# Two gated-MLP passes beside attention: ten of twelve f tiles by one level of Strassen's scheme

## The chip, the core and the metric

One core of a Trainium2 chip runs the whole program in one launch. The metric is the device time of one execution in microseconds. TensorE multiplies, VectorE, ScalarE and GpSimd do the rest, SyncE issues most DMAs; instructions on each engine run in the order in which the program holds them, and engines wait for one another by semaphores.

## What is computed

```python
q_s, k_s = q * D**-0.25, k * D**-0.25          # 4 batches, 8 heads, 576 tokens, D = 64
def phi(x):                                     # omega: 128 x 64
    h = einsum('bhsd,md->bhsm', x, omega) - sum(x * x, -1, keepdims=True) / 2
    return exp(h - max(h, -1, keepdims=True)) / sqrt(m)
kv = einsum('bhsm,bhsd->bhmd', phi(k_s), v);  z = sum(phi(k_s), axis=2)
x = einsum('bhsm,bhmd->bhsd', phi(q_s), kv) / (einsum('bhsm,bhm->bhs', phi(q_s), z)[..., None] + 1e-6)
x = x.transpose(0, 2, 1, 3).reshape(2304, 512)
x = ((x @ w_a) * (x @ w_b)) @ w_out             # 512 -> 1536 -> 512
h = maximum(x @ w_in, 0);  out = (h * h) @ w_out2   # 512 -> 2048 -> 512
```

The weights come as 64-bit floats, are read as pairs of 32-bit words and are turned into 32-bit ones on the chip.

## The kernel before

Each large product is done in three matmuls on rounded 32-bit values: an operand is cut into a high and a low part (`TERMS` lists high x high, high x low, low x high). ScalarE casts the high part, VectorE subtracts it from the value for the low part.

The 2304 tokens are nine blocks of 256. The first MLP runs in nine passes (`PASSES`, numbered from 0 here). Passes 0 to 5 take one block each, over half of the twelve f tiles (an f tile is 128 of the 1536 hidden columns); passes 6, 7 and 8 take two blocks each (3 and 4, 5 and 6, 7 and 8) over all f tiles. For an f tile the generator `a_units` yields three units: "a", twelve matmuls with w_a; "b", twelve with w_b, after which ScalarE and VectorE multiply the two results and cut the product; "o", twelve matmuls with w_out into the four y banks (`outs`), for an f tile one or two behind. In passes 6 and 7 these matmuls have 512 columns (`abw`, line 696, and `y`, line 721) and use PSUM banks 4 and 5 for w_a and w_b, 0 to 3 for y; attention has banks 6 and 7.

Attention runs beside passes 0 to 7. `SIDES` says which of its lanes go with which pass; after each unit the main loop advances them by their share. A k lane (`k_steps`, `kt_steps`) makes phi(k) and kv for one batch, a q lane (`q_steps`, `qt_steps`) makes phi(q), the quotient and the columns of x that a later pass reads. `x_all` holds two blocks, `x_mid` (from pass 6 on) blocks 5 and 6. A scheduler then sets the order of the instructions on each engine, from the order in which the program issues them and from what each needs. GpSimd issues the small loads of the last 64 tokens of each head (`kt`, `qt`, `VT`) and does nothing else after the start. w_a and w_b are all in SBUF, cut, by the end of pass 2, and w_out is kept cut in DRAM (`wo_d`) and loaded again per f tile.

The second MLP (from 634.7 us) follows the same cutting, in a scheme of seven products already; its phases are not changed but for addresses.

## Time and profile before

| | |
|---|---|
| time, median of 3 runs | 988.3 us (987.8 to 988.34) |
| profiled execution, first to last instruction | 988.2 us |
| TensorE / VectorE / ScalarE / GpSimd busy | 969.0 / 662.4 / 534.1 / 28.9 us |
| passes 3, 4, 5 | 46.0, 41.2, 42.3 us |
| passes 6, 7, 8 | 124.6, 118.2, 101.1 us |
| phases of the second MLP | 175.0 and 178.5 us |

The passes begin at 41.67, 87.42, 126.49, 161.29, 207.29, 248.47, 290.79, 415.38 and 533.55 us, each at its first matmul with w_a. Busy time of TensorE is counted to the modelled end of each matmul, so a row of starts tells more of its pace than busy time does.

### The profile page before, as it was taken

To read this page: it belongs to the slowest core of one execution; us is meant where nothing else is said; L and a number is where in the kernel's file an instruction comes from. 1 tells how busy PE (TensorE), PEld (TensorE's weight loads), DVE (VectorE), ACT (ScalarE), POOL (GpSimd) and SP (SyncE) were. 2 spreads that over 40 slices of the span, in tenths; PEclk is the share of its full clock that TensorE was granted. 3 is DMA by queue.
4 is the path that set the end of the run, shared out by engine and by line. 5 is a ranking of instruction groups with operands and counts; after the bars stand their busy time and mean duration, and the time that the engine had idled before them with its cause. 6 is when DMAs were issued, how large, how long until landed. Compare 5 with 4: busy or idle time off the path is not lost.

```text
span 988.2 us, 17329 instructions
## 1 busy us (share of the span) xinstructions
PE 969.0 (98%) x6337; PEld 890.0 (90%) x6337; DVE 662.4 (67%) x1624; ACT 534.1 (54%) x1288; POOL 28.9 (3%) x54
## 2 busy tenths in 40 slices
PE   7899999999999999999999999999999999999998
PEld 6799998999998878788888888899999999999998
DVE  3888679765544444444443998988787347988794
ACT  5876556666554533243333554676676555455561
POOL 4000100000000000000000000000000000000000
PEclk9999999999999999999999999999999999999999
DMA  7766976634553111232123999337675599844301
GB/s 188 216 177 199 296 240 210 205 100 137 156 155 101 62 57 54 70 96 76 54 65 128 310 331 362 104 107 233 215 237 200 181 363 407 355 154 145 112 18 49
DMA packets 110358, 171.07 MB, mean 173 GB/s; under 512 B 27713, under 2 KB 83521, under 8 KB 107841
## 3 DMA queue, kind: packets, MB, share of 16 engines
q1 hardware_dynamic: 108736, 168.39, 51.1%
q0 software_dynamic: 1536, 1.58, 0.6%
q8 instruction: 50, 0.82, 0.3%
q14 instruction: 36, 0.29, 0.1%
HBM read 120.13 MB, written 49.81 MB: 172 GB/s over the span
## 4 chain that ended last, share of the span: by engine, by line
PE 78%; DVE 8%; DMA 7%; ACT 5%; issue 2%; SPq 0%; ACTq 0%; DVEq 0%
PE abw L696 14%; PE y L721 10%; PE pY L1026 9%; PE oY L1184 7%; PE ab L696 7%; PE oW L1184 5%; PE pW L1026 5%; PE oX L1184 4%; PE ps_n L548 3%; PE pX L1026 2%; PE ps_kv L482 2%; PE ps_p L329 2%; PE ps_p L404 2%; DMA raw<-in_moe_w_b_dram 2%; PE ps_qt L539 2%
## 5 line engine op out<-in xcount | busy, mean ns | idle before, releaser
L696 PE MATMUL abw<-x_all,W 128*128 128x512 f32 x576 | 142.6, 395 | 0.0
L721 PE MATMUL y<-gs,wo 128*128 128x256 f32 (+1 forms) x720 | 138.1, 332 | 0.2 <-ACT wo L199 0.2
L696 PEld LDWEIGHTS abw<-x_all,W 128*128 128x128 f32 x576 | 105.7, 188 | 20.5
L721 PEld LDWEIGHTS y<-gs,wo 128*128 128x128 f32 x720 | 108.8, 189 | 11.2 <-ACT wo L199 0.6
L696 PE MATMUL ab<-x_all,W 128*128 128x256 f32 x576 | 87.5, 292 | 1.4 <-DVE W L200 0.9
L696 PEld LDWEIGHTS ab<-x_all,W 128*128 128x128 f32 x576 | 74.8, 189 | 3.0 <-DVE W L200 1.5
L696 PE MATMUL abw<-x_mid,W 128*128 128x512 f32 x288 | 71.2, 395 | 0.0
L696 PEld LDWEIGHTS abw<-x_mid,W 128*128 128x128 f32 x288 | 52.5, 188 | 10.4
L415 DVE CUSTOM_DVE_ANT_0 c<-ps_p,c 128x128 f32<-128x128 f32 x152 | 38.3, 286 | 25.0 <-ACT c L413 24.2
L802 ACT CAST gs<-a_s 128x256 fp32r<-128x256 f32 x84 | 33.0, 407 | 30.4 <-DVE a_s L801 29.2
L413 ACT COPY c<-ps_p 128x256 f32<-128x256 f32 x76 | 27.8, 372 | 36.6 <-PE ps_p L404 36.2
L1026 PE MATMUL pY<-W,M 128*128 128x384 f32 x240 | 45.9, 335 | 0.0
L801 DVE TENSOR_TENSOR a_s<-abw,a_s 128x256 f32<-128x256 f32 x48 | 18.1, 419 | 38.2 <-PE abw L696 38.2
L1184 PE MATMUL oW<-W 128*128 128x256 f32 x360 | 43.0, 276 | 0.0
L1026 PEld LDWEIGHTS pY<-W,M 128*128 128x128 f32 x240 | 41.9, 188 | 0.4 <-ACT F L1035 0.3
L1184 PEld LDWEIGHTS oW<-W 128*128 128x128 f32 x360 | 41.8, 188 | 0.2 <-DVE W L1152 0.2
L1151 ACT CAST W<-F 128x384 fp32r<-128x384 f32 x57 | 29.0, 513 | 23.5 <-PE oX L1184 10.6
L696 PE MATMUL ab<-x,W 128*128 128x256 f32 x288 | 41.3, 287 | 0.0
L800 ACT ACTIVATE a_s<-abw 128x256 f32<-128x256 f32 x48 | 17.4, 387 | 42.6 <-PE abw L696 42.5
L1043 ACT ACTIVATE F<-F 128x384 f32<-128x384 f32 x48 | 24.5, 518 | 24.8 <-DVE F L1038 24.7
L548 PEld LDWEIGHTS ps_n<-kvr,qT 128*128 128x128 f32 x256 | 32.3, 191 | 5.9 <-ACT qT L543 3.3
L420 ACT ACTIVATE qp<-c,nm 128x128 f32<-128x128 f32 x88 | 31.0, 397 | 11.4 <-DVE nm L415 10.3
(212 smaller groups left out, 2146.0 us busy)
## 6 DMA issues: line engine op xcount, KB each, us to landing
wo<-wo_d SPq DMA_DIRECT2D x60, 512.0 KB, 3.6
s_d<-F SPq DMA_DIRECT2D x24, 768.0 KB, 5.6
raw<-in_moe_w_out_dram SPq DMA_DIRECT2D x32, 256.0 KB, 4.7
raw<-in_moe_w_in_dram SPq DMA_DIRECT2D x16, 512.0 KB, 6.4
W<-wo_d SPq DMA_DIRECT2D x4, 2048.0 KB, 14.9
F<-s_d SPq DMA_DIRECT2D x5, 1536.0 KB, 7.8
raw<-in_moe_w_a_dram SPq DMA_DIRECT2D x12, 512.0 KB, 3.8
raw<-in_moe_w_b_dram SPq DMA_DIRECT2D x12, 512.0 KB, 5.2
```

Of the source, the lines that this page charges most:

```text
L329: state["proj"] = nc.tensor.matmul(ps[:, 2 * x:2 * x + 2].rearrange("p h m -> p (h m)"), lhsT=s, rhs=OMZ.rearrange("p h m -> p (h m)"), st ...
L413: nc.scalar.copy(out=c, in_=ps[:, :, 1, :])
L415: nc.vector.tensor_tensor_reduce(out=c[:, x, :], in0=ps[:, x, 0, :], in1=c[:, x, :], scale=1.0, scalar=3.0e38, op0=ALU.add, op1=ALU.min, a ...
L420: nc.scalar.activation(out=dst[:, 2 * n + x, :], in_=c[:, x, :], func=ACTF.Exp, scale=-1.0, bias=nm[:, x:x + 1],)
L548: lambda x=x: nc.tensor.matmul(pn[:, x, :], lhsT=t["qT"][:, x % 2 * len(g) + x // 2, :], rhs=kv[:, x % 2, :], start=True, stop=True,)
L696: nc.tensor.matmul(ps, lhsT=wv[:, s_, kc, :], rhs=x[..., kc, m_, :], start=(kc == 0 and (s_, m_) == TERMS[0]), stop=(kc == KC - 1 and (s_, ...
L721: nc.tensor.matmul(y_part(pi, f, c), lhsT=wo[pi, f][:, s_, c * 128:(c + 1) * 128], rhs=g[:, m_, :],  start=(f == f0 and (wide or c % 2 == ...
L802: nc.scalar.copy(out=g[:, 0, c], in_=a_s)
L1026: nc.tensor.matmul(p, lhsT=w[:, s_, 128 * kk:128 * kk + 128], rhs=y[:, ai, kk, m_, :], start=(c not in seen and kk == 0 and (s_, m_) == TE ...
L1043: nc.scalar.activation(out=t[:, o], in_=t[:, o], func=ACTF.Relu)
L1151: ahead_of["cast"] = nc.scalar.copy(out=sop[:, 0], in_=src)
L1184: nc.tensor.matmul(tiles_of(p, t), lhsT=sops[n][:, s_, 128 * t:128 * t + 128], rhs=w[:, m_, :], start=(fresh and k == 0 and (t % 2 == 0 or ...
```

## The change

In passes 6 and 7 the f tiles 0 and 1 run as before. The other ten are taken in pairs (`pair`). For a pair, x is a matrix of 2 x 2 blocks (two token blocks by two halves of the 512 inputs) and the weights one of 2 x 2 (two halves of the inputs by w_a and w_b). One level of the Strassen scheme in Winograd's form gives the four results from seven block products. They need sums of blocks on both sides:

- sums of x (`sums_of_x`): s1, s2, s4, and s3 in place of a block of x, on VectorE and ScalarE while f tiles 0 and 1 run;
- sums of w (`t_made`): four per f tile, by GpSimd in passes 3 and 4, cut by ScalarE and VectorE, stored in DRAM (`t_d`, 1 MB per f tile) and loaded (`t_load`) 512 KB at a time, three buffers, in passes 6 and 7.

The seven products of a pair go through banks 4 and 5 (`sP`, `sR`); each is twelve matmuls of 256 columns. Partial results are copied out or added as they come. The cut product lies in one buffer (`g_mid`). Pools are laid out anew: what only k lanes use is in a pool of its own that closes before pass 6, so all of batch 3's k lane moves into pass 5 (half of it ran in pass 6). Some addresses and pads differ.

```diff
+    def t_made(f):
+        w = seg("W", 8192 * f, 2, 2, 512)
+        full = top["cut"].tile([128, 2, 2, 256], F32, tag="a", name="a")
+        nc.gpsimd.tensor_tensor(
+            out=full.rearrange("p a r n -> p a (r n)"), in0=f32(w[:, :, 0]), in1=f32(w[:, :, 1]),
+            op=ALU.add,
+        )
+        yield
+        b11, b21, b12, b22 = (full[:, a, r] for a in range(2) for r in range(2))
+        t = top["cut"].tile([128, 4, 256], F32, tag="p", name="p")
+        for o, x, y in ((0, b12, b11), (2, b22, b12), (1, b22, t[:, 0]), (3, b21, t[:, 1])):
+            nc.gpsimd.tensor_tensor(out=t[:, o], in0=x, in1=y, op=ALU.subtract)
+        yield
+        o = top["raw"].tile([128, 4, 2, 256], F32R, tag="raw", name="raw")
+        nc.scalar.copy(out=o[:, :, 0], in_=t)
+        nc.vector.tensor_tensor(out=o[:, :, 1], in0=t, in1=f32(o[:, :, 0]), op=ALU.subtract)
+        nc.sync.dma_start(out=t_d[f // 2 - 1][:, :, f % 2], in_=f32(o))
+        yield
...
+        def sums_of_x(x):
...
+            tt(first, u, hi(a21), hi(a22), ALU.add)
+            tt(first, u, u, lo(a21), ALU.add)
+            tt(first, u, u, lo(a22), ALU.add)
+            cut(first, s1, u)
...
+        def pair(pi, f, x, n0):
...
+            prod(p, a11, old(wa, 0), first=True)
+            nc.scalar.copy(out=e1, in_=p)
+            prod(r, s1, new(0), first=True)
+            nc.scalar.copy(out=e5, in_=r)
+            t_load(n0 + 3)
+            yield pi, f, "a"
+            prod(p, s2, new(1))
+            nc.scalar.copy(out=e2, in_=p)
+            t_load(n0 + 4)
+            prod(r, s4, old(wb, 1), last=True)
+            nc.vector.tensor_tensor(out=e2, in0=r, in1=e2, op=ALU.add)
+            yield pi, f, "b"
+            outs(*pending.pop(0))
+            yield pi, f, "o"
+            prod(p, s3, new(2))
+            nc.vector.tensor_tensor(out=e5, in0=p, in1=e5, op=ALU.add)
+            t_load(n0 + 5)
+            r = bank(5, [128, 2, N], "sR")
+            prod(r, a12, old(wa, 1), first=True, last=True)
+            nc.vector.tensor_tensor(out=e1, in0=r, in1=e1, op=ALU.add)
+            nc.vector.scalar_tensor_tensor(
+                out=e1, in0=e1, scalar=1.0 / W_SCALE, in1=e2, op0=ALU.mult, op1=ALU.mult
+            )
+            yield pi, f + 1, "a"
+            prod(p, a22, new(3), last=True)
+            nc.vector.scalar_tensor_tensor(
+                out=e5, in0=p, scalar=1.0 / W_SCALE, in1=e5, op0=ALU.mult, op1=ALU.mult
+            )
+            t_load(n0 + 6)
+            yield pi, f + 1, "b"
+            outs(*pending.pop(0))
...
-        5: lambda: merge(q_lane(2, (0,)), k_lane(3, (0, 1))),
+        5: lambda: merge(q_lane(2, (0,)), k_lane(3)),
         6: lambda: chain(
-            merge(q_lane(2, (1, 2)), k_lane(3, (2, 3))),
+            q_lane(2, (1, 2)),
...
+        if T_FROM <= pi < AT_END - 1 and (kind != "a" or f % 3):
+            next(t_work, None)
```

On TensorE, in pass 7, before: `abw` is a product with w_a or w_b of one f tile, `ps_` names are attention, `y0` and on the w_out product.

```order
L404 MATMUL ps_p_5461<-OM_127,S_5426 128x256 x2
L696 MATMUL abw_5470<-x_mid_3999,W_107 128x512 x12
L561 MATMUL ps_x_5484<-ident_125,xh_5454 128x128 x2
L404 MATMUL ps_p_5490<-OM_127,S_5426 128x256 x2
L696 MATMUL abw_5471<-x_mid_3999,W_107 128x512 x12
L539 MATMUL ps_qt_5524<-ident_125,qp_5459 128x128 x4
L721 MATMUL y0_5431<-gs_5405,wo_5354 128x512 x3
```

The same pass now, the last three products of one pair, then (after the w_out products left out here) the first two of the next:

```order
L580 MATMUL ps_n_5918<-kvr_3793,qT_5890 128x65 x4
L854 MATMUL sP_5810<-x_mid_4268,tsum_5579 128x256 x12
L854 MATMUL sR_5943<-x_mid_4268,W_115 128x256 x12
L436 MATMUL ps_p_5960<-OM_138,S_5913 128x256 x2
L593 MATMUL ps_x_5969<-ident_136,xh_5923 128x128 x2
L854 MATMUL sP_5810<-x_mid_4268,tsum_5838 128x256 x12
...
L854 MATMUL sP_6022<-x_mid_4268,W_115 128x256 x12
L854 MATMUL sR_6023<-xs1_4272,tsum_5868 128x256 x12
```

Chains of twelve stay, but they have half the columns, alternate between two banks, and some follow one another with nothing between.

On GpSimd, in passes 3 and 4, now (`a` and `p` are the sums of w for one f tile, `kt` the small loads of k); before, the loads stand there alone:

```order
L248 TENSOR_TENSOR a_3255<-W_115 128x1024
L339 DMA kt_3550<-in_k_dram 64x2x64 x4
L256 TENSOR_TENSOR p_3286<-a_3255 128x256 x2
L256 TENSOR_TENSOR p_3286<-a_3255,p_3286 128x256 x2
L248 TENSOR_TENSOR a_3369<-W_115 128x1024
```

The loads keep their order among themselves and get sums ahead of them.

On VectorE, at the start of pass 7, now (`gu` and `xs1` are sums of x):

```order
L799 TENSOR_TENSOR gu_5603<-x_mid_4268 128x512
L799 TENSOR_TENSOR gu_5603<-gu_5603,x_mid_4268 128x512 x2
L803 TENSOR_TENSOR xs1_4272<-gu_5603,xs1_4272 128x2x256
L799 TENSOR_TENSOR gu_5603<-gu_5603,x_mid_4268 128x512
L967 TENSOR_TENSOR a_s_5635<-abw_5605,a_s_5635 128x256
L967 TENSOR_TENSOR a_s_5638<-abw_5605,a_s_5638 128x256
L398 TENSOR_TENSOR S_5646<-ps_t1_5643,S_5646 64x256
```

Instructions of the product (`a_s`) and of attention (`S`) stand among them in one queue.

## Rows read from the trace of the kernel before

**Rows 1.** Page, busy time by engine: us (share of span) and instructions
```profile
PE 969.0 (98%) x6337; PEld 890.0 (90%) x6337; DVE 662.4 (67%) x1624; ACT 534.1 (54%) x1288; POOL 28.9 (3%) x54
```
**Rows 2.** Stretches of passes 3 to 8: length, busy (instructions), clock, DMA share, GB/s
```profile
core 0: us, PE busy (x) PEld busy (x) DVE busy (x) ACT busy (x) POOL busy (x), PEclk, DMA share, GB/s
161.29:207.29 46.00, 45.34 (x367) 43.18 (x366) 35.01 (x130) 29.94 (x88) 1.17 (x2) 1.00 0.58 182
207.29:248.47 41.18, 40.81 (x330) 38.70 (x329) 23.69 (x102) 23.72 (x74) 3.49 (x6) 1.00 0.40 122
248.47:290.79 42.32, 42.13 (x345) 40.22 (x344) 23.38 (x101) 24.49 (x75) 0.00 (x0) 1.00 0.55 164
290.79:415.38 124.59, 124.31 (x645) 101.83 (x644) 56.67 (x219) 49.24 (x152) 2.32 (x4) 1.00 0.22 69
415.38:533.55 118.17, 118.17 (x602) 98.87 (x600) 48.39 (x177) 43.70 (x127) 0.00 (x0) 1.00 0.26 83
533.55:634.67 101.12, 100.96 (x446) 83.25 (x444) 89.01 (x154) 52.78 (x81) 0.00 (x0) 1.00 0.81 281
```
**Rows 3.** Waits of TensorE in passes 3 to 7, longest: us, times, longest
```profile
PE ps_p L404 <- DVE S L367: 0.4, 2, 0.2
PE ps_xt L616 <- DVE xh L524: 0.3, 1, 0.3
```
**Rows 4.** Order of time on TensorE, passes 7 and 8: start, length, what
```profile
425.37 2.93 PE L696 MATMUL abw<-x_mid,W 128*128 128x512 f32 x12
428.13 0.40 PE L404 MATMUL ps_p<-OM,S 128*128 128x256 f32 x2
428.37 2.93 PE L696 MATMUL abw<-x_mid,W 128*128 128x512 f32 x12
431.14 0.60 PE L539 MATMUL ps_qt<-ident,qp 128*128 128x128 f32 x4
...
566.19 5.60 PE L696 MATMUL abw<-x_all,W 128*128 128x512 f32 x24
571.63 0.62 PE L721 MATMUL y<-G,wo 128*128 128x512 f32 x2
```
**Rows 5.** Order of time on TensorE, pass 5
```profile
258.72 1.66 PE L721 MATMUL y<-gs,wo 128*128 128x256 f32 x12
260.22 0.27 PE L379 MATMUL ps_t<-ident,qn 128*128 128x128 f32 x1
260.25 1.66 PE L696 MATMUL ab<-x,W 128*128 128x256 f32 x12
261.75 0.60 PE L329 MATMUL ps_p<-OMZ,T 128*128 128x256 f32 x2
```
**Rows 6.** Stretch of the last phase, line 1184 (256 columns) alone
```profile
809.70:988.20 178.50, 173.49 (x1512) 1.00 0.49 184
```
**Rows 7.** Groups by line and shape: busy us, mean ns of one
```profile
L200 DVE TENSOR_TENSOR W<-p,W 128x1024 fp32r<-128x1024 f32 x12 | 14.7, 1224 | 3.7 <-ACT W L199 3.4
L199 ACT CAST W<-p 128x1024 fp32r<-128x1024 f32 x12 | 12.6, 1050 | 2.5 <-DVE p L195 2.4
L803 DVE TENSOR_TENSOR G<-F,G 128x512 fp32r<-128x512 f32 x12 | 8.2, 684 | 1.2 <-ACT G L802 1.2
L750 DVE SCALAR_TENSOR_TENSOR y_p<-y,y_p 128x512 f32<-128x512 f32 x6 | 4.1, 683 | 0.0
L742 ACT ACTIVATE y_s<-y 128x512 f32<-128x512 f32 x8 | 4.8, 599 | 7.0 <-PE y L721 5.5 <-DMA y_d<-y_s 1.4
```
**Rows 8.** Page, DMA issues: KB each, us to landing
```profile
wo<-wo_d SPq DMA_DIRECT2D x60, 512.0 KB, 3.6
```
**Rows 9.** Stretches within pass 3, columns as in rows 2
```profile
161.29:176.60 15.31, 14.65 (x114) 13.45 (x113) 14.56 (x38) 9.08 (x24) 0.00 (x0) 1.00 0.59 197
176.60:207.29 30.69, 30.69 (x255) 29.73 (x254) 20.45 (x93) 20.86 (x65) 1.17 (x2) 1.00 0.58 174
```
**Rows 10.** Order of time on GpSimd
```profile
2.11 0.31 POOL masks.py:199 TENSOR_SCALAR_AFFINE_SELECT ident<-ident 128x128 f32<-128x128 f32 x1
...
214.89 2.32 POOL L307 DMA_DIRECT2D kt<-in_k_dram x4 [23.14 <-PE ps_tt L317]
```
**Rows 11.** Groups of passes 3 to 5
```profile
L420 ACT ACTIVATE kp<-c,nm 128x128 f32<-128x128 f32 x48 | 16.8, 398 | 3.2 <-DVE nm L415 3.0
```

More of the change, by code (lines that the diff above doesn't have):

```diff
@@ L111 @@
     wo_d = [dram.tile([128, 2, 512], F32, name=f"wo_d{f}") for f in range(FA)]
+    t_d = [dram.tile([128, 4, 2, 2, 256], F32, name=f"t_d{i}") for i in range(1, FA // 2)]
     y_d = [
@@ L475, in k_steps @@
         yield
-        kp = ap1.tile([128, 8, M], F32, tag="kp", name="kp")
+        kp = apk.tile([128, 8, M], F32, tag="kp", name="kp")
         for i in range(0, 4, 2):
@@ L757, in outs, with tt, cut @@
                 nc.sync.dma_start(out=y_cols(i)[:, c:c + 2, :], in_=t)
+        def sums_of_x(x):
+            a11, a12, a21, a22 = x[:, 0, 0:2], x[:, 0, 2:4], x[:, 1, 0:2], x[:, 1, 2:4]
+            s1, s2, s4 = (top["s"][i] for i in (1, 2, 4))
+            hi, lo = (lambda t, m=m: f32(t[:, :, m]) for m in range(2))
+            first, then = [], []
+            def tt(ops, o, x, y, op):
+                ops.append(lambda: nc.vector.tensor_tensor(out=o, in0=x, in1=y, op=op))
+            def cut(ops, t, u):
+                ops.append(lambda: nc.scalar.copy(out=t[:, :, 0], in_=u))
+                ops.append(lambda: nc.vector.tensor_tensor(
+                    out=t[:, :, 1], in0=u, in1=hi(t), op=ALU.subtract
+                ))
+            u = f32(gpool.tile([128, 2, N], F32R, tag="gs", name="gu"))
+            tt(first, u, hi(a21), hi(a22), ALU.add)
+            tt(first, u, u, lo(a21), ALU.add)
+            tt(first, u, u, lo(a22), ALU.add)
+            cut(first, s1, u)
+            tt(first, u, u, hi(a11), ALU.subtract)
+            tt(first, u, u, lo(a11), ALU.subtract)
+            cut(first, s2, u)
+            tt(first, u, hi(a12), u, ALU.subtract)
+            tt(first, u, u, lo(a12), ALU.add)
+            cut(first, s4, u)
+            tt(then, u, hi(a11), hi(a21), ALU.subtract)
+            tt(then, u, u, lo(a11), ALU.add)
+            tt(then, u, u, lo(a21), ALU.subtract)
+            cut(then, a21, u)
+            return first, then
@@ L768, in a_units @@
             wide = len(bl) == 2
+            fast = wide and pi <= AT_END
+            if fast:
+                at = (pi - AT_END + 1) * 4 * len(t_d)
+                if f == 0:
+                    if not t_now:
+                        for i in range(3):
+                            t_load(i)
+                    first, then = sums_of_x(x_pair(bl[0]))
+                if f >= 2:
+                    if f % 2 == 0:
+                        yield from pair(pi, f, x_pair(bl[0]), at + (f - 2) * 2)
+                    continue
             if wide:
@@ L778, in a_units @@
             proj(aps, wa[f], x)
+            if fast:
+                for _ in range(3):
+                    if first:
+                        first.pop(0)()
             yield pi, f, "a"
             proj(bps, wb[f], x)
+            if fast and f == 1:
+                while first or then:
+                    (first or then).pop(0)()
             if wide:
@@ L1283 @@
     }
+    T_FROM = 3
     FR = {0: 0.7, 6: 0.95, 7: 0.9}
@@ L1352, in begin @@
         if pi == AT_END - 1:
+            for _ in t_work:
+                pass
             top["st"].close()
             x2st.close()
-            open_area("raw", 8384, I32, "right", pa)
+            kctx.close()
             open_mid()
@@ L1361, in begin @@
             open_area("F", 24576, F32)
+    t_work = (x for f in range(2, FA) for x in t_made(f))
     begin(0)
```

151 lines of the change are left out of this document (114 added, 37 removed).

## The prediction

> **What bounds the kernel now.** I read the engine totals first, then the stretches of the passes, the waits of TensorE, and last the order of time inside a pass. TensorE is busy 98% of the span [rows 1], and the passes say the same stage by stage: in passes 3 to 8 it stands idle 0.0 to 0.7 us each, at a granted clock of 1.00, which is 2.4 GHz [rows 2]. In passes 3 to 7 its two longest waits come to 0.7 us together [rows 3]. VectorE is busy 45% and 41% of passes 6 and 7, ScalarE 40% and 37%. So in passes 6 and 7, where the products are changed, the end is set by how many columns TensorE streams and by what each matmul costs beyond its columns. Pass 8 is the same work without attention: 101.1 us against 124.6 and 118.2, so attention costs TensorE some 23 and 17 us there. The times below are made against the span of 988.2 us; the median of the runs, 988.3, lies 0.1 above it.
>
> **The products.** Before, a pair of f tiles takes 2 x 2 x 12 = 48 matmuls of 512 columns. Now it takes seven products of 12 matmuls of 256 columns, 84 in all: 21,504 columns for 24,576, seven eighths. There are five pairs in each of two passes.
>
> What a matmul costs is read from start to start, since the ends are modelled. In pass 7 twelve of 512 columns, begun after an attention piece, run from 425.37 to 428.13 and from 428.37 to 431.14, 2.765 us or 230 ns each; in pass 8, without attention, 24 run from 566.19 to 571.63, 227 ns each [rows 4]. For 256 columns, twelve between attention pieces run from 258.72 to 260.22 and 260.25 to 261.75, 1.50 us or 125 ns each [rows 5]; in the last phase, where nothing interrupts, 1512 take 173.49 us, 115 ns each [rows 6]. So a 256-column chain pays some 0.1 us for each restart.
>
> Before: 48 x 230 ns = 11.06 us a pair. After, by the two ends: 84 x 125 = 10.50 if each product is restarted, 84 x 115 = 9.66 if none is. The gain is 0.56 to 1.40 us a pair, 5.6 to 14.0 us for ten pairs. The new order has an attention piece or a y group ahead of about four of the seven products, the other three follow directly: 4 x 1.50 + 3 x 1.38 = 10.14, a gain of 0.92. That is in the middle of both ends; I take 9.5 us, rounding up a little because the 512-column chains of pass 6 meet more attention than those of pass 7.
>
> **The chain within a pair.** All seven products go through two banks, so evictions now stand between products. The tightest: the fifth product's sum is added out of bank P by VectorE before the seventh may write there. Such an instruction of 512 columns takes 683 ns, a ScalarE eviction 599 [rows 7]; the sixth product covers it with 1.38 to 1.50 us, some 0.7 us to spare. Per pair VectorE has 7 instructions of 684 ns for 8 of 0.42, ScalarE 5 of 0.6 for 8 of 0.4. A wait arises only where an attention instruction stands ahead: 0 to 0.5 us a pair; I take 0.1, 1 us for ten. The four loads of sums a pair, 512 KB each like the wo loads that land in 3.6 us [rows 8], come from three buffers ahead, some 14 us at one load in 4.8 us. On SyncE each load waits for TensorE to be done with its buffer, with a wo load and a q load queued behind it; these have buffers ahead too. I cost the loads at nothing; without that cover it would be a few us each.
>
> **The sums of x.** At the start of passes 6 and 7 VectorE gets 14 instructions of 512 elements, 14 x 0.684 = 9.6 us [rows 7], and ScalarE 4 casts, within the first two f tiles and the end of the pass ahead, some 20 us. With attention and evictions at the 45% of pass 6 that makes 18.6 of 20 us. A stretch so full is shown: from 161.29 to 176.60 VectorE is busy 14.56 of 15.31 us and TensorE idle 0.66, while after it, at 20.45 of 30.69, TensorE is never idle [rows 9]. So 4% of 20 us, 0.75 us a pass, 1.5 for both. Bounds 0 and 4: the drain of the y banks by ScalarE falls in the same place in pass 7.
>
> **The sums of w in passes 3 and 4.** For each of ten f tiles GpSimd does one add of 1024 elements and four subtractions of 256, ScalarE a cast of 1024, VectorE a subtraction of 1024, SyncE a store of 1 MB. No row shows GpSimd adding. The nearest is one pass over 128 elements in 311 ns [rows 10]: by count of elements the five instructions are at most 16 x 0.311 = 5.0 us a tile, by count of instructions 1.6. Nothing but the ScalarE cast waits for it, and that is issued one step (some 2.5 us) after the subtractions; the add of the next tile runs ahead. GpSimd thus has 8 us a tile. ScalarE gets 10 x 1.05 = 10.5 us, 53.7 to 64.2 of 87.2; VectorE 10 x 1.224 = 12.2 [rows 7], 58.7 to 70.9, or 81%, in part just where it is at 95% already. I charge 1.5 us, between 0 and 4% of 87.2 us, 3.5.
>
> The GPSIMD Engine Reference of the Trainium skill (section 3.1) puts an add of 2048 fp32 values at 4.5 us; an estimate from it is 2.2 us for the add and 0.56 for each subtraction, 4.5 us a tile, within the ends above. No run here shows it.
>
> On GpSimd the loads of kt and VT now stand behind sums, up to 5 us later; the kt load for pass 5, which begins at 248.47, went out at 214.89 [rows 2, 10], so I cost this at nothing.
>
> **Pass 5.** The second half of the last batch's k work moves from pass 6 into pass 5, because its pool closes earlier. For TensorE this is a shift of some 9 us, not a gain. But pass 5 then has 66 attention steps in 18 units for 45. Its ScalarE work, 24.49 us of 42.32 [rows 2], grows by about 13 us (the 48 exponentials of six such steps take 16.8, so those of two 5.6 [rows 11]; the copies and casts about as much again), to 37 of 52 us. The later part of pass 3 runs at such a share without idle time. I charge 1 us, 0 to 2.5.
>
> **Sum.** -9.5 + 1 + 1.5 + 1.5 + 1 = -4.5: the span goes to 983.7, the median to 983.8. By the ends of every term: -14.0 with no charge is 974.3; -5.6 with 0.5 x 10 + 4 + 3.5 + 2.5 = 15 is 997.7.
>
> **Rivals.**
> A. The restarts eat the gain. Every product pays its restart, 84 x 125 ns: -5.6 + 5 = -0.6, 987.7 us. For it: all 12-chains of rows 5 pay it. Against: three of seven products stand directly behind another.
>
> B. Slower: VectorE becomes the bound of passes 3 and 4. It has 22 instructions there with both inputs in SBUF (12 of the products' low parts, 10 of the sums). If each must wait until a GpSimd instruction that reads SBUF is done, the wait is up to half of the add's 2.5 us, 1.25 us, 27 us in all: 70.9 + 27.5 = 98.4 us of work in 87.2, so 11.2 us more. With the gain and the other charges that is -9.5 + 11.2 + 3.5 = +5.2, 993.5 us. It decides from (87.2 - 70.9) / 22 = 0.74 us a wait. Against: GpSimd is busy for at most 5.0 of 8.7 us, most of its instructions are the short ones, so the mean wait is nearer 0.4 us, 9 us of VectorE. The trace of before has no GpSimd arithmetic and bears out neither. SBUF — State Buffer of the Trainium skill (section Who interferes with whom) has such a rule: a VectorE instruction with two SBUF inputs contends with a GpSimd one that reads SBUF, and the first to start keeps the shared pair for all of its duration. By that rule the low parts, now 0.42 us, would show longer in these passes.
>
> C. All is covered. The waits stay as rare as now and the products run near the pace of the last phase: -14.0 + 1 = -13.0, 975.3; with the middle gain and no charges 978.8. For it: the order keeps TensorE fed in passes 3 to 7 today with the other engines at up to 95%.
>
> D. Slower: the two banks are a chain. If evictions come late by one attention instruction plus their own time in each half of a pair, 0.6 us twice, ten pairs lose 12 us: -9.5 + 12 + 4 = +6.5, 994.8. Against it: before, bank pairs are freed through ScalarE and VectorE as well and TensorE's waits in these passes are near zero.
>
> **How the numbers follow.** Two executions can be told apart by about 0.2%, 2 us. Forecast (980 to 986.3): 0.41. A (986.3 to 990.3): 0.17. B: 0.13. C (below 980): 0.21. D: 0.08. The forecast and C are faster, and a small part of A; B and D are slower, with a part of A. Faster 0.64, same 0.14, slower 0.22. The range 975 to 993 leaves out the outer parts of B, C and D; the forecast's own is 980 to 986.3.
>
> **What would show it.** Passes 6 and 7 together, now 242.8 us, less the 9 us moved, should come to some 226 to 229, with 256-column chains of 1.38 to 1.50 us and TensorE waits on the evictions under 0.3 us a pair. Passes 3 and 4, now 87.2, should stay under 90; low parts clearly above 0.42 us and passes of 95 us would be B. Pass 5 should be 51 to 53. Waits of TensorE on evictions of sP or sR over 1 us a pair would be D. I am wrong in kind if passes 6 and 7 fall by much more than the columns tell, or if stages after pass 7 move by over 1 us.

## The result, and the profile after

The changed kernel takes 1000.35 us in the median of four runs (997.13 to 1001.42), the kernel before 988.32 beside it: 1.0106 times, 95% interval 1.0082 to 1.0131. It is slower, by 12 us; 983.8 was forecast, with a range up to 993. The two profiled spans are 988.2 and 999.7 us.

The stages of the changed kernel, as stretches of its trace: start, end and length, busy time (instructions) of PE, PEld, DVE, ACT, POOL, PE's granted clock, DMA share, GB/s. The rows are passes 3 to 8 and the two later phases, and answer to [rows 2, 6]:

```profile
159.90:212.96 53.06, 43.60 (x330) 40.40 (x328) 43.59 (x103) 28.39 (x72) 32.97 (x32) 0.97 0.67 226
212.96:257.52 44.56, 42.42 (x344) 40.29 (x343) 35.82 (x123) 30.29 (x86) 24.91 (x27) 1.00 0.78 250
257.52:310.50 52.98, 52.68 (x423) 49.71 (x422) 33.45 (x150) 35.71 (x113) 0.00 (x0) 1.00 0.50 144
310.50:423.03 112.53, 111.39 (x766) 99.30 (x764) 66.00 (x203) 42.72 (x117) 2.33 (x4) 1.00 0.54 171
423.03:535.82 112.79, 112.79 (x775) 103.34 (x774) 63.37 (x178) 45.89 (x114) 0.00 (x0) 1.00 0.48 155
535.82:641.98 106.16, 106.16 (x458) 85.52 (x457) 85.61 (x151) 51.62 (x79) 0.00 (x0) 1.00 0.86 294
641.98:817.88 175.90, 175.74 (x1009) 174.95 (x1008) 127.03 (x229) 118.89 (x253) 0.00 (x0) 1.00 0.59 205
817.88:999.65 181.77, 177.60 (x1513) 176.48 (x1512) 144.93 (x286) 88.69 (x176) 0.00 (x0) 1.00 0.48 179
```

The first later phase of the kernel before, in the same view:

```profile
634.67:809.65 174.98, 174.98 (x1009) 174.70 (x1008) 122.56 (x223) 116.12 (x249) 0.00 (x0) 1.00 0.60 205
```

Passes 3 and 4 went from 87.2 to 97.6 us. Passes 5 to 8 went from 386.2 to 384.5, a gain of 1.7 where 6 was forecast. The first later phase lost 0.9 us, the last one 3.3, though no instruction of TensorE was added there. What comes ahead of pass 3 is 1.4 us shorter, which tells nothing: in the eighteen profiles of this study it takes 159.4 to 165.9 us, whatever the kernel.

**Passes 3 and 4.** TensorE now stands idle 9.5 and 2.1 us of the two passes. One view tells of a tile's instructions: duration in ns, minimum/median/maximum, first and last start. The tile is the one that holds a sum's high and low parts:

```profile
L260 DVE TENSOR_TENSOR raw<-p,raw x10: 1209/2269/2443, 180.8 to 248.5; 128x1024 fp32r<-128x1024 f32 x10
```

And line 994, the low part of a product, after, and the same instruction (line 803) before:

```profile
L994 DVE TENSOR_TENSOR gs<-a_s,gs x13: 407/426/2278, 166.6 to 257.3; 128x256 fp32r<-128x256 f32 x13
```
```profile
L803 DVE TENSOR_TENSOR gs<-a_s,gs x13: 405/423/426, 168.0 to 246.8; 128x256 fp32r<-128x256 f32 x13
```

An instruction of 1224 ns [rows 7] takes 2269, one of 423 up to 2278. GpSimd's order of time shows beside what (start, length, instruction, idle time before it and what ended it):

```profile
172.06 2.38 POOL L248 TENSOR_TENSOR a<-W 128x1024 f32<-128x1024 f32 x1 [12.78 <-DVE p L197]
...
179.77 2.40 POOL L248 TENSOR_TENSOR a<-W 128x1024 f32<-128x1024 f32 x1
183.39 1.41 POOL L256 TENSOR_TENSOR p<-a 128x256 f32<-128x256 f32 x2 [1.23 <-DVE raw L260]
```

The add of the next tile starts at 179.77. VectorE's low part starts at 180.80, is held until the add ends at 182.17, and ends at 183.25 (the chain below); only then may GpSimd subtract again. The Trainium skill (SBUF — State Buffer, section Who interferes with whom) says that such a VectorE instruction contends with a GpSimd one that reads SBUF, and that the first to start keeps the shared pair; these rows agree. The chain of waits is the same loop, over and over (start, length, what):

```profile
179.72 1.06 ACT raw L259
...
180.80 2.45 DVE raw L260
...
183.39 2.11 POOL p L256 x3
...
186.33 1.06 ACT raw L259
```

That is 6.6 us a tile; the casts of the first five tiles follow one another 6.6 to 6.8 us apart, the later ones 5.8 to 12.1. The waits in these two passes that belong to the loop, TensorE's longest wait there (us in all, times, longest), and TensorE in steps of 5 us:

```profile
POOL p L256 <- DVE raw L260: 11.2, 8, 2.4
ACT raw L259 <- POOL p L256: 8.2, 5, 3.3
PE y L753 <- DVE y_p L782: 2.4, 1, 2.4
```
```profile
180.00:185.00 5.00, 2.59 (x20) 2.39 (x20) 4.14 (x10) 2.27 (x6) 3.77 (x4) 0.96 0.38 140
185.00:190.00 5.00, 4.11 (x22) 3.73 (x20) 3.25 (x7) 2.48 (x6) 3.62 (x4) 0.70 0.95 333
```

ScalarE waits 8.2 us for subtractions, and evictions and attention steps stand queued behind it. On VectorE they stand behind the held low part: `y_p`, for which TensorE waits 2.4 us until 184.39, starts at 183.66, after that low part has ended at 183.25. TensorE, busy 2.59 of 5 us, then gets a granted clock of 0.70 over the next 5, so part of them at 1.2 GHz.

**The pace of the matmuls.** TensorE's order of time at the start and in the middle of pass 8 now, answering to [rows 4], and at its start before:

```profile
535.82 5.76 PE L728 MATMUL abw<-x_all,W 128*128 128x512 f32 x24
541.41 5.75 PE L753 MATMUL y<-g_mid,wo 128*128 128x512 f32 x24
...
563.77 5.76 PE L728 MATMUL abw<-x_all,W 128*128 128x512 f32 x24
569.37 2.96 PE L753 MATMUL y<-G,wo 128*128 128x512 f32 x12
```
```profile
533.55 5.60 PE L696 MATMUL abw<-x_all,W 128*128 128x512 f32 x24
538.99 2.88 PE L721 MATMUL y<-gs,wo 128*128 128x512 f32 x12
```

Twenty-four products take 569.37 - 563.77 = 5.60 us, 233 ns each; before they took 227. Nothing waits there. The rows at the start show a second thing: a pair leaves two y groups over at its end, the old order one, so 12 matmuls, 2.8 us, moved from ahead of pass 8 into it. Of the 5.0 us that pass 8 grew, 2.2 are pace.

In the last phase the pace changes within the stage, at a restart:

```profile
860.13 4.24 PE L1375 MATMUL oW<-W 128*128 128x256 f32 x36
864.21 1.18 PE L1375 MATMUL oW<-W,M 128*128 128x256 f32 x9
865.23 3.60 PE L1375 MATMUL oW<-W 128*128 128x256 f32 x27
...
870.78 4.40 PE L1375 MATMUL oY<-Q,W 128*128 128x256 f32 x36
875.02 1.22 PE L1375 MATMUL oY<-Q,M 128*128 128x256 f32 x9
```

At 860.13 36 matmuls take 4.08 us, 113 ns each; after a wait within the 27 at 865.23 (two of them start 0.27 and 0.22 us after the one before), 36 take 4.24 us, 118 each, and it stays so until 988: some 1000 matmuls by 4.5 ns.

### The profile page after: what moved, and what is told of

It is laid out like the page before. It is cut to its first block, busy times and chain, and to the rows that moved or that the text cites. A ratio compares the mean times of both kernels' runs of the same rounds, so it can differ in the third digit from the quotient of the medians.

```text
span 999.7 us, 18241 instructions
## 1 busy us (share of the span) xinstructions
PE 970.4 (97%) x6697; PEld 906.4 (91%) x6697; DVE 719.2 (72%) x1652; ACT 547.6 (55%) x1276; POOL 82.1 (8%) x104
## 4 chain that ended last, share of the span: by engine, by line
PE 83%; DVE 6%; ACT 6%; POOL 2%; issue 2%; DMA 1%; SPq 0%; DVEq 0%; ACTq 0%; POOLq 0%
PE y L753 12%; PE pY L1217 10%; PE abw L728 9%; PE oY L1375 8%; PE ab L728 6%; PE sP L854 5%; PE pW L1217 5%; PE oX L1375 5%; PE oW L1375 4%; PE sR L854 4%; PE ps_n L580 3%; PE pX L1217 3%; PE ps_p L361 2%; PE ps_kv L514 2%; PE ps_p L436 2%
## 5 line engine op out<-in xcount | busy, mean ns | idle before, releaser
L728 PE MATMUL abw<-x_all,W 128*128 128x512 f32 x336 | 82.3, 397 | 0.8 <-ACT a_s L966 0.8
L728 PEld LDWEIGHTS abw<-x_all,W 128*128 128x128 f32 x336 | 62.7, 188 | 15.7 <-ACT a_s L966 1.0
L753 PE MATMUL y<-g_mid,wo 128*128 128x512 f32 x288 | 74.9, 401 | 0.0
L753 PE MATMUL y<-gs,wo 128*128 128x256 f32 x432 | 67.7, 292 | 2.8 <-DVE y_p L782 2.4
L753 PEld LDWEIGHTS y<-gs,wo 128*128 128x128 f32 x432 | 57.2, 191 | 4.0 <-DVE y_p L782 2.6
L753 PEld LDWEIGHTS y<-g_mid,wo 128*128 128x128 f32 x288 | 51.8, 189 | 9.9
L728 PE MATMUL ab<-x,W 128*128 128x256 f32 x288 | 46.9, 290 | 0.0
L1342 ACT CAST W<-F 128x384 fp32r<-128x384 f32 x57 | 29.0, 513 | 24.7 <-PE oX L1375 13.5
L728 PEld LDWEIGHTS ab<-x,W 128*128 128x128 f32 x288 | 39.3, 190 | 0.1
L580 PE MATMUL ps_n<-kvr,qT 128*128 128x65 f32 x256 | 35.0, 274 | 3.4 <-ACT qT L575 2.5
L436 PE MATMUL ps_p<-OM,S 128*128 128x256 f32 x152 | 34.4, 308 | 3.8 <-DVE x L655 1.5
```

The costliest lines, as they stand in the source:

```text
L436: lambda ps=ps, o_=o_, x=x: nc.tensor.matmul(ps[:, x].rearrange("p a m -> p (a m)"), lhsT=self.s[:, x, o_:o_ + 128], rhs=OM.rearrange("p a ...
L580: lambda x=x: nc.tensor.matmul(pn[:, x, :], lhsT=t["qT"][:, x % 2 * len(g) + x // 2, :], rhs=kv[:, x % 2, :], start=True, stop=True,)
L728: nc.tensor.matmul(ps, lhsT=wv[:, s_, kc, :], rhs=x[..., kc, m_, :], start=(kc == 0 and (s_, m_) == TERMS[0]), stop=(kc == KC - 1 and (s_, ...
L753: nc.tensor.matmul(y_part(pi, f, c), lhsT=wo[pi, f][:, s_, c * 128:(c + 1) * 128], rhs=g[:, m_, :],  start=(f == f0 and (wide or c % 2 == ...
L1342: ahead_of["cast"] = nc.scalar.copy(out=sop[:, 0], in_=src)
```

## Experiments

All stages run from the first matmul of one to the first of the next, in us, from one profiled execution; the time is the run's, or the median where there are several (the changed kernel, 14 and 15). The kernel before, on the same chips, took 987.9 to 990.6 in the median, 987.8 to 993.1 in single runs; so a few us between single runs tell little, and the stages tell more.

| kernel | time | 3+4 | 5 | 6+7 | 8 | first later | last |
|---|---|---|---|---|---|---|---|
| before | 988.3 | 87.2 | 42.3 | 242.8 | 101.1 | 175.0 | 178.5 |
| changed | 1000.35 | 97.6 | 53.0 | 225.3 | 106.2 | 175.9 | 181.8 |
| 1 before, shifted 64 bytes | 996.0 | 87.4 | 42.4 | 244.8 | 103.3 | 175.4 | 179.0 |
| 2 stores alone | 988.8 | 87.1 | 50.0 | 225.2 | 106.2 | 175.9 | 177.7 |
| 3 unread sums | 994.9 | 91.4 | 53.0 | 225.3 | 106.2 | 175.9 | 181.8 |
| 4 spread | 995.0 | 99.1 | 50.4 | 225.2 | 106.2 | 175.9 | 177.1 |
| 5 no GpSimd | 988.5 | 84.8 | 53.0 | 225.4 | 106.2 | 175.9 | 182.0 |
| 6 short adds | 996.6 | 96.4 | 53.0 | 225.3 | 106.2 | 175.9 | 177.1 |
| 7 aligned | 995.2 | 97.6 | 53.0 | 223.9 | 104.7 | 175.6 | 178.1 |
| 8 sums by VectorE | 997.7 | 94.8 | 53.9 | 224.8 | 106.2 | 175.9 | 177.1 |
| 9 late start | 999.4 | 98.7 | 52.7 | 225.4 | 106.2 | 175.9 | 177.9 |
| 10 late, short adds | 1001.0 | 99.7 | 52.8 | 225.4 | 106.2 | 175.9 | 177.6 |
| 11 aligned, late | 994.6 | 98.4 | 52.8 | 223.8 | 104.2 | 175.6 | 177.6 |
| 12 cast one later | 1010.6 | 111.0 | 50.7 | 225.4 | 106.2 | 176.0 | 177.1 |
| 13 the same, short adds | 1008.7 | 111.7 | 50.7 | 225.3 | 106.2 | 175.9 | 177.2 |
| 14 the same, aligned | 1007.0 | 112.2 | 50.7 | 223.9 | 104.2 | 175.6 | 178.0 |
| 15 aligned, no GpSimd | 981.4 | 85.0 | 53.0 | 224.1 | 104.2 | 175.6 | 178.0 |
| 16 unread, short adds | 991.9 | 92.0 | 53.0 | 225.4 | 106.2 | 176.0 | 177.1 |

**1. Is it the addresses?**

```diff
-    edge.tile([128, 8], F32, name="edge")
+    edge.tile([128, 24], F32, name="edge")
```


> The kernel before, with one number changed: a pad at the right end of SBUF grows by 64 bytes, so that x, the R area and what else lies at the right end stand 64 bytes lower against the weights. No work changes. Theory 1 (the pace of a matmul chain follows the distance in SBUF between its moving and its stationary operand): pass 8 goes from 101.1 us to about 106, its 512-column matmuls from 227 to 233 ns from start to start, and the first later phase from 175.0 to about 176, as in the changed kernel. Theory 2 (the pace of the changed kernel came from its heavier DMA traffic or from the new work in passes 6 and 7): pass 8 stays at 101.1 within 0.3, the later phase at 175.0 within 0.3.

Sixty-four bytes of padding make the kernel before about 8 us slower, by one run of each; in the profiles it is 5.3 us from pass 3 on. Pass 8 grew by 2.2, not 5: I had not yet seen the 2.8 us of moved y work. Its products:

```profile
570.10 5.76 PE L696 MATMUL abw<-x_all,W 128*128 128x512 f32 x24
575.70 2.96 PE L721 MATMUL y<-G,wo 128*128 128x512 f32 x12
```

They take 5.60 us from start to start, the changed kernel's 233 ns, with the DMA share at 0.79. Theory 1 holds, theory 2 falls. The first later phase comes to 175.4, not 176: this padding makes less than half of its 0.9 us.

**2. Stores alone.** Both GpSimd steps and ScalarE's and VectorE's go.

```diff
-        nc.sync.dma_start(out=t_d[f // 2 - 1][:, :, f % 2], in_=f32(o))
+        w = seg("W", 8192 * f, 4, 2, 256)
+        nc.sync.dma_start(out=t_d[f // 2 - 1][:, :, f % 2], in_=f32(w))
```


> The changed kernel without the making of the sums of w: in passes 3 and 4 only the 10 stores of 1 MB to DRAM are left, and they store the weights themselves, so the products take weights in place of sums. GpSimd, ScalarE and VectorE lose this work. Theory 1 (the sums cost passes 3 and 4 their 10.4 us): passes 3 and 4 together go from 97.6 us to 87 to 89, and everything from pass 5 on stays within 1 us. Theory 2 (the loss there is the new layout, the stores or the pace of the matmuls): they stay above 94 us.

87.1 us: theory 1. Without the sums passes 3 and 4 lose nothing. The later stages did not all stay within 1 us: pass 5 is 3.0 us shorter, which kernel 5 explains, and the last phase 4.1, by the two paces above. The run stands at 988.8, no better than before, but 3.7 us of that lie ahead of pass 3, which the edit leaves alone; from pass 3 on it is 4.8 us shorter than the kernel before.

**3. Unread sums.**

```diff
-        nc.scalar.copy(out=o[:, :, 0], in_=t)
+        z = f32(seg("W", 8192 * f, 4, 2, 256)[:, :, 0])
+        nc.scalar.copy(out=o[:, :, 0], in_=z)
```


> The changed kernel with the same GpSimd sums, but nobody reads them: ScalarE's cast and VectorE's low part take the weights in their place, so neither waits for GpSimd, and GpSimd does not wait for them. Same number and size of instructions on every engine. Theory 1 (the price is VectorE held while GpSimd runs, rival B of the prediction): VectorE's instructions with two SBUF inputs are as long as now (the low part of 1024 elements 2.3 us in the median) and passes 3 and 4 stay at 95 to 98 us. Theory 2 (the price is the chain GpSimd, ScalarE, VectorE, GpSimd, in whose waits both engines let the products' evictions stand): these two passes come down to 88 to 91 us although VectorE's instructions stay long.

91.4 us, close to theory 2's 88 to 91: 6.2 us go with the waits for GpSimd; what is left is the matter of kernel 5. I expected held instructions as long as before; the median fell to 1470 ns, but the longest is 3250:

```profile
L261 DVE TENSOR_TENSOR raw<-W,raw x10: 1212/1470/3250, 176.1 to 242.1; 128x1024 fp32r<-128x1024 f32 x10
```

**5. No GpSimd.** As kernel 3, without the five GpSimd instructions a tile.

```diff
-        nc.gpsimd.tensor_tensor(
-            out=full.rearrange("p a r n -> p a (r n)"), in0=f32(w[:, :, 0]), in1=f32(w[:, :, 1]),
-            op=ALU.add,
-        )
...
-            nc.gpsimd.tensor_tensor(out=t[:, o], in0=x, in1=y, op=ALU.subtract)
```


> The changed kernel without the GpSimd sums: ScalarE's cast and VectorE's low part are still made, from the weights themselves, and stored. So the same two instructions and the store a tile as with unread sums, but GpSimd idle. With unread sums passes 3 and 4 took 91.4 us, with the stores alone 87.1. Theory 1 (VectorE held by GpSimd): low parts of 1024 elements at 1.22 us in the median, those of 256 at 0.42, passes 3 and 4 at 87 to 88.5 us. Theory 2 (ScalarE and VectorE have too much to do there, with or without GpSimd): 90.5 to 92 us, as with unread sums.

84.8 us, and every low part takes its own time: theory 1, though below its 87 to 88.5. Passes 3 and 4 here, in kernel 3, and in kernel 2:

```profile
159.40:244.20 84.80, 82.80 (x671) 79.24 (x670) 66.38 (x225) 58.45 (x158) 4.68 (x8) 1.00 0.80 273
```
```profile
159.70:251.06 91.36, 84.25 (x671) 79.44 (x670) 78.02 (x225) 58.76 (x158) 65.48 (x58) 1.00 0.75 253
```
```profile
164.97:252.04 87.07, 86.24 (x693) 81.89 (x694) 59.02 (x229) 54.61 (x162) 4.66 (x8) 1.00 0.59 190
```

With the same 225 instructions VectorE is busy 11.6 us longer beside GpSimd (kernel 3), and the passes take 6.6 us longer. TensorE's waits in kernel 3 are for VectorE and ScalarE, none for a load that GpSimd issues. So holding alone costs 6.6 us, and the chain 6.2 more, 12.8 in all. Against the kernel before it was 10.4, and 84.8 lies below 87.1, because the work in the stretches differs: kernel 2's row has 693 matmuls, those of 5 and 3 have 671. In these and the changed kernel the scheduler puts attention matmuls of pass 4 into pass 5, which takes 53.0 us in place of 50.0. Passes 3 to 5 together take 137.1 us in kernel 2, 137.8 in 5, 144.3 in 3 and 150.6 in the changed kernel. So the sums cost 13.5 us: 6.3 by the chain, 6.5 by holding, and 0.7 is left for what ScalarE and VectorE do for them.

**4, 6, 9 and 10. Spacing.** The steps in fewer units, the add in four pieces, the steps from the third f tile of pass 3 on, and the last two together.

```diff
-        if T_FROM <= pi < AT_END - 1 and (kind != "a" or f % 3):
+        if T_FROM <= pi < AT_END - 1 and (kind == "o" or kind == "b" and f % 3 == 0):   # 4
+        if pi == 3 and f >= 8 or pi == 4:                                               # 9, 10
...
+        for y, r in ((0, 0), (1, 0), (1, 1), (0, 1)):                                   # 6, 10
+            c = slice(256 * r, 256 * r + 256)
+            nc.gpsimd.tensor_tensor(
+                out=full[:, y, r], in0=f32(w[:, y, 0, c]), in1=f32(w[:, y, 1, c]), op=ALU.add
+            )
```


> The changed kernel with the 30 steps of the sums of w issued in 32 of the 72 units of passes 3 and 4 in place of 64: one step every 2.6 us or so in place of 1.3. Same work. Theory 1 (VectorE held by GpSimd): each instruction is held as before, passes 3 and 4 stay at 95 to 98 us. Theory 2 (the chain of waits): the cast is issued some 2.6 us behind the subtractions, the engines wait less, and the two passes come down to 90 to 93 us.

The edit isn't what I expected of it: the two passes have 36 units, not 72, so 14 of the 30 steps were left to be issued at the start of pass 5. Nor did it space the work: the scheduler put the sums nearly where they had been, the first add 12.1 us into pass 3 (12.2 in the changed kernel), the last at 244.5 us and the last cast at 254.6, before pass 5 begins at 258.4. At 99.1 us it tells nothing for either theory.

> The changed kernel with GpSimd's add of 1024 elements (2.39 us) cut into four of 256 (0.75 us each, 3.0 us a tile in place of 2.4). Theory 1 (VectorE is held until the GpSimd instruction that runs is over): no VectorE instruction is held for more than 0.75 us, the low part of 1024 elements comes from 2.3 us to below 2.0, passes 3 and 4 from 97.6 to 92 to 95 us. Theory 2 (GpSimd slows VectorE by its share of the port, however its work is cut): 97 to 99 us, since GpSimd works 6 us longer. Theory 3 (the chain of waits alone): unchanged or 1 us longer.

No VectorE instruction of this form is over 1.66 us now, the median 1460 ns:

```profile
L261 DVE TENSOR_TENSOR raw<-p,raw x10: 1225/1460/1659, 181.1 to 248.5; 128x1024 fp32r<-128x1024 f32 x10
```

Yet the passes gain only 1.2 us, between the ranges of theories 1 and 2. ScalarE's waits for GpSimd grew from 8.2 to 13.6 us, as the loop a tile did not get shorter.

> The changed kernel with its 30 steps of the sums of w issued from the third f tile of pass 3 on, one in every unit (12 in pass 3, 18 in pass 4), in place of one in most units from the start of pass 3. Same work. In the changed kernel GpSimd's first add waits 12.8 us for the last cut of w_out, whose two tiles it shares, and GpSimd stays behind the program from then on, so that ScalarE and VectorE wait for it in their own order. Theory 1 (that lag is the price of the chain): GpSimd's first wait goes below 3 us, ScalarE's waits for the subtractions from 8.2 us in all to under 3, and passes 3 and 4 from 97.6 to 90 to 93 us (91.4 with unread sums). Theory 2 (GpSimd's work beside VectorE costs it, wherever it starts): 95 to 98 us.

98.7 us, theory 2 by its number; ScalarE waits 13.2 us for the subtractions. But the edit did not take away the lag that it was to take away: the scheduler lets GpSimd's first add wait 12.8 us for the last cut of w_out as before and start 12.2 us into pass 3, as in the changed kernel, and so it is in kernels 10 to 14. Whether that lag has a part in the price is not shown. GpSimd's order of time shows what lengthens a loop here:

```profile
230.74 2.36 POOL L339 DMA_DIRECT2D kt<-in_k_dram  x4 [3.18 <-PE ps_tt L349]
233.11 1.63 POOL L256 TENSOR_TENSOR p<-a 128x256 f32<-128x256 f32 x2
234.70 1.53 POOL L256 TENSOR_TENSOR p<-a,p 128x256 f32<-128x256 f32 x2
```

GpSimd first waits 3.2 us for TensorE to free the kt buffer, with the subtractions queued behind that load; the subtractions run until 236.2, and TensorE is busy 2.67 us of the 5 from 236.

> The late start and the short adds together: four GpSimd adds of 256 in place of one of 1024. Theory 1 (with the lag gone, what is left is VectorE held by GpSimd, by the length of its instructions): 1 to 3 us less in passes 3 and 4 than the late start alone, 87 to 91 us. Theory 2 (holding costs nothing once the lag is gone, since VectorE has time): the same as the late start within 1 us, or longer by GpSimd's 6 us of additional work.

99.7 us, theory 2: while the chain is there, shorter holds give nothing.

**12, 13 and 14. The cast one tile later.** GpSimd writes into the tile that is stored; its cast and low part are issued a tile later. Kernel 12 has the late start of 9, 13 the short adds, 14 the addresses of 11 as well.

```diff
-        t = top["cut"].tile([128, 4, 256], F32, tag="p", name="p")
+            o = top["raw"].tile([128, 4, 2, 256], F32R, tag="raw", name="raw")
+            t = f32(o[:, :, 1])
...
+            if late:
+                rest(*late)      # copy, low part and store of the tile before
+            late = f, o
```


> The late start again, but GpSimd writes its differences straight into the two buffers that the store reads, so that it need not wait for VectorE's low part of the tile before, and ScalarE's cast and VectorE's low part of a tile are issued one whole tile after its subtractions. Same work, same number of steps. Theory 1 (6 us of the loss are ScalarE and VectorE standing in their own order for GpSimd): ScalarE's waits for GpSimd go from 13.2 us to under 2, GpSimd's for VectorE from 8.3 to under 2, passes 3 and 4 from 98.7 to 90 to 93 us, as with unread sums (91.4), though VectorE is still held. Theory 2 (the price is GpSimd running beside VectorE, and the waits only show it): 95 to 99 us.

Both theories fall: 111.0 us. One wait took another's place. GpSimd now waits for a buffer whose store has not landed:

```profile
198.87 1.43 POOL L264 TENSOR_TENSOR raw<-a 128x256 f32<-128x256 f32 x2 [9.07 <-DMA t_d<-raw]
```

> As the kernel with the cast one tile later, with GpSimd's add of 1024 elements in four of 256. Theory 1 (what is left once the chain is gone is VectorE held for the length of a GpSimd instruction): the low part of 1024 elements comes below 1.45 us in the mean and passes 3 and 4 to 87 to 91 us, 1 to 4 less than without the cut. Theory 2 (being held costs nothing by itself): the same within 1 us.

> The cast one tile later and the short adds, with the addresses of the aligned kernel with the late start. If both causes stand as found: passes 3 and 4 at 87 to 91 us, passes 6 and 7 at 223.8, pass 8 at 104.2, the first later phase at 175.6, the last at 177 to 179; in all 983 to 988 us, 0 to 5 us below the kernel before. If the chain is not the cause: 993 to 996, as with the late start and aligned addresses (994.6).

111.7 and 112.2 us in passes 3 and 4; the new wait hides what they were to tell. Kernel 14 takes 1.0181 times the kernel before (1.0164 to 1.0198); pass 8 and the first later phase come as expected, 104.2 and 175.6.

**8. Sums by VectorE.**

```diff
-        nc.gpsimd.tensor_tensor(
+        nc.vector.tensor_tensor(
```


> The changed kernel with the sums of w made by VectorE in place of GpSimd. VectorE then has 59 us as with the stores alone, and 10 times 1.22 + 1.22 + 4 x 0.42 us, 41 us, in all 100 us in passes that TensorE needs 87 for. Theory 1 (being held costs VectorE about as much as it saves): its busy time, 79.4 us now, goes to 95 to 100 and passes 3 and 4 to 98 to 103 us. Theory 2 (the two engines together are what costs, not the work): below 95 us.

94.8 us, theory 2: VectorE, busy 85.3 us in place of 79.4, does the sums itself, and the passes are 2.8 us shorter than with GpSimd's help. The last tile's subtractions and low part come in pass 5; passes 3 to 5 together are 2.0 us shorter, 148.6 for 150.6.

**16. Unread sums, short adds.** Kernel 3 with the adds of kernel 6.

> The kernel with unread sums, where no engine waits for GpSimd, with GpSimd's add of 1024 elements in four of 256. Theory 1 (the 4 to 6 us between no GpSimd work, 84.8 to 87.1 us, and unread sums, 91.4, are VectorE held until a long GpSimd instruction ends): low parts of 1024 elements from 2.3 us to under 1.7 in the median, and passes 3 and 4 to 87 to 90 us. Theory 2 (they go by GpSimd's busy time, which grows by 6 us): 91 to 93 us.

92.0 us, theory 2 by its number. The rows say why, and are the surprise of the study. VectorE and GpSimd here (start, length, instruction), and TensorE beside them:

```profile
236.81 2.80 POOL L250 TENSOR_TENSOR a<-W 128x256 f32<-128x256 f32 x4
237.70 5.03 DVE L262 TENSOR_TENSOR raw<-W,raw 128x1024 fp32r<-128x1024 f32 x1
239.57 1.39 POOL L257 TENSOR_TENSOR p<-a 128x256 f32<-128x256 f32 x2
240.93 2.38 POOL L257 TENSOR_TENSOR p<-a,p 128x256 f32<-128x256 f32 x2
```
```profile
239.00:244.00 5.00, 1.39 (x11) 1.15 (x10) 4.91 (x6) 0.31 (x1) 4.92 (x7) 0.87 0.62 227
244.00:252.00 8.00, 8.00 (x49) 8.00 (x48) 4.18 (x19) 4.05 (x12) 2.76 (x5) 0.66 0.68 230
```

A VectorE instruction that starts at 237.70 ends at 242.73. Five GpSimd instructions that were queued behind the running one went ahead of it, with no gap between them. TensorE, busy 1.39 of 5 us, then has a clock of 0.66 for 8 us; this one hold and what the clock took after it are most of what this kernel loses. At the 252nd of the 288 matmuls with w_a and w_b in the two passes, just ahead of the hold, it is 1.3 us behind kernel 5, where kernel 3 is 6.6 behind; at their end it is 7.2 behind. So up to there theory 1 is right, and the number alone misleads. A hold does not always end with the GpSimd instruction that runs when VectorE comes, and neither theory had that. It is the exception: the run's other nine low parts took 1.2 to 1.8 us, though GpSimd is busy 34.33 of the 35 us from 204 to 239. What lets several instructions past stays open.

**7 and 11. Addresses alone, and with the late start.**

```diff
-    edge.tile([128, 48], F32, name="edge")
+    edge.tile([128, 32], F32, name="edge")
...
+    x_all, x_8 = (x_mem[:, o:o + XN].rearrange(...) for o in (0, 16))   # x_8 in pass 8
...
+        gm.tile([128, 48], F32, name="g_pad")
-        x56.tile([128, 112], F32, name="x_pad")
+        x56.tile([128, 64], F32, name="x_pad")
-        tp.tile([128, 80], F32, name="t_pad")
+        tp.tile([128, 48], F32, name="t_pad")
...
-                g = seg("G", 4096 * (f % 2), 2, 2 * N)
+                g = seg("G", 64 + 4096 * (f % 2), 2, 2 * N)    # 192 in kernel 11
```


> The changed kernel with addresses alone changed: the distance between moving and stationary operand, modulo 256 bytes, becomes 0 or 128 for the 512-column matmuls of pass 8 and of y in passes 6 and 7 (192 or 64 now), 192 for all 256-column products of the pairs (64, 128, 0 or 192 now), 0 for all 384-column matmuls of the first later phase (0 or 192 now), and in the last phase every fifth weight tile is at 64 again (192 now). Theory 1 (the pace goes by that distance): pass 8 106.2 to about 101.2 us, the first later phase 175.9 to 175.0, passes 6 and 7 225.3 to 219 to 223, the last phase 177 to 179; passes 3 and 4 as now (97 to 99). In all 988 to 992. Theory 2 (address has no part in it, the loads of the pairs or the chip's state set the pace): pass 8 stays at 106 and passes 6 and 7 at 225.

> The late start, with the addresses of the aligned kernel, and G 128 bytes further so that y in pass 8 too has its operands at a distance of 0 modulo 256 (it had 128 there, and 232 ns from start to start). Theory 1 (pace by distance modulo 256, and the lag): y in pass 8 at 227 ns, pass 8 at 101 to 101.5 us (104.65 with G at 128), passes 3 and 4 as with the late start alone, 90 to 93; in all 983 to 987 us, below the kernel before. Theory 2 (the 128 has no part; y is slow for its loads): pass 8 stays at 104 to 105 us and the whole at 986 to 990.

Kernel 11 differs by G's offset and the late start. Kernel 7 came to 995.2, above the 988 to 992 expected, and passes 6 and 7, pass 8 and the first later phase fell short of the gains expected, but each moved the right way: passes 6 and 7 by 1.4 us, pass 8 by 1.5, the first later phase by 0.3. Rows of pass 8 in 7, then in 11:

```profile
551.50 2.95 PE L758 MATMUL y<-G,wo 128*128 128x512 f32 x12
554.28 5.64 PE L733 MATMUL abw<-x_all,W 128*128 128x512 f32 x24
```
```profile
546.35 5.64 PE L733 MATMUL abw<-x_all,W 128*128 128x512 f32 x24
551.83 2.89 PE L758 MATMUL y<-G,wo 128*128 128x512 f32 x12
554.56 5.64 PE L733 MATMUL abw<-x_all,W 128*128 128x512 f32 x24
```

In kernel 11 the products take 5.48 us for 24, 228 ns (233 in the changed kernel). The y group takes 2.78 us, 232 ns, at a distance of 128 (kernel 7), and 2.73, 228, at 0. The 104.2 of kernel 11 is the 101.1 of before and the 2.8 us of y moved, and 0.3 more: pass 8 is explained. By its number kernel 11's pass 8 is theory 2's, 104 to 105; by its rows, y at 228 in place of 232, it is theory 1's: the expectation of 101 had left the moved work out. Its passes 3 and 4, 98.4 us where 90 to 93 were expected, keep the whole at 994.6.

**15. Both causes taken away.** Kernel 5 with the addresses of kernel 11.

> The changed kernel without the GpSimd sums (cast and low part made from the weights, as in the kernel without GpSimd) and with the addresses of the aligned kernel with the late start: both causes found are taken away, the products, their loads and the sums of x stay. If the two causes are the whole loss: passes 3 and 4 at 85 to 87 us, passes 6 and 7 at 223.8, pass 8 at 104.2, the last phase at 177 to 178; in all 980 to 984 us, 5 to 9 below the kernel before, near the 983.8 forecast. If something else ate the gain as well: 986 or more.

981.4 us in the median of four, 0.9909 times the kernel before (0.9877 to 0.9941). Its profiled execution, at 987.4, has a pass 1 of 44.0 us, 37.7 to 40.0 in all the others; the stages from pass 3 on are as expected. From there on it is 20.0 us shorter than the changed kernel: 12.6 in passes 3 to 5, by the sums; 3.6 in passes 6 to 8 and the first later phase, by the addresses; 3.8 in the last phase, of whose two paces it has the shorter. The first two are the causes found; the third is not explained (see the end).

## Why the prediction was wrong

**The sums of w in passes 3 and 4: the step that failed.** I charged 1.5 us between 0 and 3.5; it was 10.4 in the two passes, and 13.5 with the attention matmuls that moved from pass 4 into pass 5 (kernel 2). The work was nearly of the size assumed: 2.4 us for the add and 0.7 to 0.8 for a subtraction, 5.4 us a tile, against the 5.0 of my upper end. The estimate from the Trainium skill (GPSIMD Engine Reference, section 3.1) was 4.5: right for the add, 2.2 to 2.4, and short for the subtractions, 0.56 to some 0.75. What failed is "Nothing but the ScalarE cast waits for it, and that is issued one step (some 2.5 us) after the subtractions". The cast waits in ScalarE's order with the evictions behind it, the low part in VectorE's, and GpSimd in turn waits for the low part and stands behind the kt and VT loads. I had asked what the sums delay in GpSimd's queue, and not what that queue delays in the sums. A stretch that is 4% idle at 95% busy [rows 9] says nothing of a loop through three engines that work in order.

**Rival B** had the right place and nearly the right sum, 11.2 us; the time that it gave, 993.5, lacks the pace. Its mechanism is about half: holding alone costs 6.6 us (kernels 5 and 3), the waits for GpSimd 6.2 (kernel 3 and the changed one). But VectorE did not become the bound: it is busy 79.4 of 97.6 us, 13.0 more than in kernel 5, which is 0.6 us for each of the 22 waits, below B's 0.74 and not far from my 0.4. What I had wrong in the case against B is what such a wait costs: it counts by what stands behind the held instruction, as `y_p` did for TensorE, and not by VectorE's sum.

**The products and pass 5.** Forecast for passes 5 to 7 was -9.5 + 1 + 1.5 + 1 = -6.0. Their stretches fell by 6.8, but 2.8 of that is the y group that moved into pass 8, and some 3 us of attention came into pass 5 from pass 4. Kernel 14 has the addresses set and all but two of the matmuls of before in passes 3 and 4 (691 start there, 693 before), and its passes 5 to 8 together take 378.8 us, 386.2 before: -7.4. The mechanism was right and the gain a little larger than forecast: in pass 7 a product of twelve takes 462.26 to 463.68, 1.42 us, within my 1.38 to 1.50:

```profile
462.26 1.58 PE L854 MATMUL sR<-xs,tsum 128*128 128x256 f32 x12
463.68 0.60 PE L571 MATMUL ps_qt<-ident,qp 128*128 128x128 f32 x4
```

**The chain within a pair and the sums of x.** TensorE's only wait of note in passes 6 and 7 is this one; D falls, and both charges were too high:

```profile
PE abw L728 <- ACT a_s L966: 0.8, 1, 0.8
```

**After pass 7 nothing should have moved.** The prediction named this as the sign that it is wrong in kind. Pass 8 paid 2.2 us by pace, the later phases 0.9 and 3.3; of the 0.9 the aligned kernel gives back 0.3, and the rest is open, as is the 3.3. The sum had no term for this: the diff shows every pad that slows pass 8, and I read them as bookkeeping.

**A and C.** Restarts did not eat the gain, so A falls. With the sums for nothing and the addresses set (kernel 15), 981.4 lies between the 983.8 forecast and C, within the forecast's own 980 to 986.3; that run is of a kernel without the sums and bears out the products, not the forecast. No version that makes the sums and reads them beats the kernel before: the nearest is kernel 11, at 994.6.
